# Holding back output transposes, moving an eviction to ScalarE and three subtractions to GpSimd in a one-core attention and gated-cosine kernel

## The chip, the core and the metric

The kernel runs on one core of one Trainium2 chip. A core has TensorE for matrix products (PE in the profile, its weight loads PEld), VectorE (DVE), ScalarE (ACT), GpSimd (POOL) and SyncE (SP), which here issues most of the DMAs. The engines run side by side, each works through its own instructions in the order in which the program gives them, and semaphores make one wait for another. The metric is the device time of a run in microseconds (us), the median of several runs; lower is better.

## The reference

Two parts follow each other. A recurrent cross attention lets 512 tokens and 32 state vectors of each of 8 heads read each other, for 8 batches. Its result, 544 rows for each batch and 4352 in all, goes through a layer with the activation h·cos(h):

```python
B, H, S, Ns, D = (8, 8, 512, 32, 64)
a     = softmax(scale * x @ state.T)        # (B, H, S, Ns)
xread = a @ state
a2    = softmax(scale * state @ x.T)        # (B, H, Ns, S)
sread = a2 @ x
attn_out = concatenate([xread, sread], axis=2)           # 512 + 32 rows for a batch
x = attn_out.transpose(0, 2, 1, 3).reshape(B * 544, 512)
h = x @ w_in          # (4352, 512) @ (512, 2048)
g = h * cos(h)
out = g @ w_out       # (4352, 2048) @ (2048, 512)
```

## The kernel before

The second layer works with transposed data: features lie on partitions, the 512 tokens of a batch in the free dimension. A *step* makes one tile of h, 128 of the 2048 features (f = 0 to 15) for one batch, and turns it into a tile of g. So a batch has 16 steps, and the 32 x 8 = 256 state rows follow in 16 steps at the end.

Two batches form a pair (n = 0 to 3), because the product g @ w_out is done for two batches at once with seven block products in place of eight. A pair has four phases of eight steps: phases 0 and 1 are the even batch, phases 2 and 3 the odd one, and i = 0 to 7 counts the steps of a phase. For this, sums and differences of g tiles are made as the tiles come. The g tiles of phases 0 to 2 are also made two at a time with seven products in place of eight (`seven`, from batch 2 on); phase 3 of each pair uses the plain form below.

```python
hps = ctx.enter_context(tc.tile_pool(name="hps", bufs=2, space=PSUM))
osb = ctx.enter_context(tc.tile_pool(name="osb", bufs=2))
NHELD = 3

def hidden(t):                       # L471: the hidden product
    t.hp = hps.tile([P, S], F32, name="h")[:, 0:t.n]
    for i in range(t.kn):
        nc.tensor.matmul(out=t.hp, lhsT=t.lhs(i), rhs=t.rhs(i), ...)

# h cos h: turns of h are rounded to whole ones, the rest goes through the sine
def gate(t):                         # L567, ScalarE
    nc.scalar.activation(t.q.bitcast(I32), t.hp, func=ACTF.Copy, bias=0.25)
def gate2(t):                        # L570, VectorE
    nc.vector.tensor_tensor(t.q, t.q.bitcast(I32), t.hp, op=ALU.subtract)
def gate3(t):                        # L573, ScalarE
    nc.scalar.activation(t.q, t.q, func=ACTF.Sin, bias=halfpi, scale=-TWO_PI)
def gate4(t):                        # L580, VectorE: g, and the last reader of h
    nc.vector.tensor_tensor(t.g, t.hp, t.q, op=ALU.mult)

def minus(pr, out, a, b, soon=False):        # L586
    engine = nc.vector if soon and pr.n else nc.gpsimd
    engine.tensor_tensor(out, a, b, op=ALU.subtract)

def plus(out, bank, ch, b):                  # L630, VectorE, reads a PSUM bank
    ...
def keep_product(out, bank):
    nc.scalar.activation(out.t[:, 0], acc[bank][0], func=ACTF.Copy, scale=TWO_PI)         # L635
    nc.vector.tensor_scalar(out.t[:, 1], acc[bank][1], TWO_PI, None, op0=ALU.mult)        # L637
```

A finished output stands transposed in a `held` buffer. `store` puts two closures into a list, and the loop over the steps takes one of them in each step:

```python
later = []
def store(b, half, src):
    def go(ch):
        ot = osb.tile([P, S], F32, name="ot")
        nc.vector.transpose(out=ot..., in_=src.t[:, ch]...)      # L651
        for q in range(P // 32):
            nc.sync.dma_start(out=rows[:, :, c0:c0 + 32], in_=ot[32 * q:32 * q + 32]...)   # L657
        src.done()
    later.extend([lambda: go(0), lambda: go(1)])

def sums(t):
    pr, i = t.pair, t.i
    pr.b[t.phase, i] = t
    if t.phase == 2:
        minus(pr, pr.b[0, i].g, t.g, pr.b[0, i].g, True)         # t1
    if t.phase == 3:
        minus(pr, pr.b[0, i].g, t.g, pr.b[0, i].g, True)
        minus(pr, pr.b[2, i].g, t.g, pr.b[2, i].g)

def output(t):                       # three steps after its tile
    ...
    if t.phase < 3 and pr.before and i % 3 < 2:
        pr.before.more(1)            # two products left over from the pair before
    ...
    if t.phase == 2:
        if product(MAIN, s1, pr.b[0, i], i):     # the fifth product; true after i = 7
            pr.p5 = Held()
            keep_product(pr.p5, MAIN)
    ...
```

The last of the products that the pair before left over comes with i = 4 of phase 2, in step 7 of the odd batch; then `plus` and `store` follow. At the same time the attention of the next batch is computed, as parts that a plan gives to the steps: for an odd batch b, the scores and `max1` in step 5, `spread1` (L339) and `shift` (L356) in step 6, `max2` (L349) and both exponentials (L360, L365) in step 7, sums (L333, L375, L376) and `spread1` (L339) in step 8, `norm1` (L386) in step 9. In step 11 `halves` (L493) makes sums for the next batch's hidden products, in step 12 `keep` (L419) follows. The main loop, cut:

```python
for step, t in enumerate(all_tiles):
    s = step % NF
    ...
    hidden(t)                        # or the form for two tiles
    ...
    go(0)                            # parts of the attention
    gate(t); gate2(t)
    go(1); go(3)
    gate3(t)
    ...
    if later:
        later.pop(0)()
    ...
    gate4(t)
    if t.pair is not None:
        sums(t)
    go(2); go(4)
    ...
    while len(line) >= (LAG if step >= 2 * NH else LAG + 1):     # LAG = 3
        output(line.pop(0))
    line.append(t)
```

Of the kernel before, what the change touches and what calls it, by code (L numbers as in the profile page):

```python
# [13 lines left out]
ACTF = mybir.ActivationFunctionType  # L14
# [3 lines left out]
TWO_PI = 2.0 * math.pi  # L18
# [3 lines left out]
def kernel(  # L22
# [8 lines left out]
    nc = tc.nc  # L31

    B, H, S, D = x.shape
# [9 lines left out]
    scale = 1.0 / math.sqrt(D)  # L43
# [23 lines left out]
    NH = NF // 2  # L67
# [58 lines left out]
    def load_state(half, queues):  # L126
        b = slice(4 * half, 4 * half + 4)
        for k in range(NK):
# [11 lines left out]
    acc = [[ops.tile([P, S], F32, name=f"o{m}{ch}") for ch in range(2)]  # L140
           for m in range(2)]
# [109 lines left out]
    class Attention:  # L251
# [126 lines left out]
        def sums(self):  # L378
            self.reduce1([self.z1[:, j] for j in range(2)], ALU.add)
            self.inverse(self.m1 if self.b == 0 else self.i12)  # L380
# [98 lines left out]
    def seven(t):  # L479
        return t.pair is not None and t.b > 1 and t.phase < 3  # L480
# [103 lines left out]
# [4 lines that stand above are left out]
    MAIN, SIDE = 0, 1  # L588
# [33 lines left out]
    def product(bank, w, g, i):  # L622
        for ch in range(2):
            nc.tensor.matmul(out=acc[bank][ch],  # L624
                             lhsT=w[:, i, P * ch:P * ch + P], rhs=g.g,
                             start=(i == 0), stop=(i == NH - 1))
        return i == NH - 1

    def plus(out, bank, ch, b):
        nc.vector.scalar_tensor_tensor(out=out.t[:, ch], in0=acc[bank][ch],  # L630
                                       scalar=TWO_PI, in1=b.t[:, ch],
                                       op0=ALU.mult, op1=ALU.add)

    def keep_product(out, bank):
        nc.scalar.activation(out.t[:, 0], acc[bank][0], func=ACTF.Copy,  # L635
                             scale=TWO_PI)
        nc.vector.tensor_scalar(out.t[:, 1], acc[bank][1], TWO_PI, None,  # L637
                                op0=ALU.mult)

    later = []  # L640
# [6 lines left out]
# [4 lines that stand above are left out]
            nc.vector.transpose(out=ot.rearrange("p (j i) -> p j i", i=32),  # L651
                                in_=src.t[:, ch].rearrange(
                                    "p (j i) -> p j i", i=32))
            rows = out[b * T:b * T + S, :].rearrange("(j t) d -> t j d", t=32)
            for q in range(P // 32):
                c0 = HD * half + P * ch + 32 * q
                nc.sync.dma_start(  # L657
                    out=rows[:, :, c0:c0 + 32],
                    in_=ot[32 * q:32 * q + 32].rearrange(
                        "p (j i) -> p j i", i=32))  # L660
# [5 lines that stand above are left out]
        pr, i = t.pair, t.i  # L666
        pr.b[t.phase, i] = t
        if t.phase == 2:
            minus(pr, pr.b[0, i].g, t.g, pr.b[0, i].g, True)
        if t.phase == 3:  # L670
            minus(pr, pr.b[0, i].g, t.g, pr.b[0, i].g, True)
            minus(pr, pr.b[2, i].g, t.g, pr.b[2, i].g)
# [6 lines left out]
    def free(t):  # L679
        g_free.append(t.slot)  # L680
# [18 lines left out]
    def output(t):  # L699
        if t.pair is None:  # L700
            state_output(t)
            return
        pr, i = t.pair, t.i
        if t.phase < 3 and pr.before and i % 3 < 2:
            pr.before.more(1)
        if t.phase == 0:
            if product(MAIN, a11, t, i):
                pr.u = Held()
                keep_product(pr.u, MAIN)
        if t.phase == 1:  # L710

            bank = MAIN if pr.before else SIDE
            if product(bank, a12, t, i):
                o = Held()
                for ch in range(2):
                    plus(o, bank, ch, pr.u)
                store(2 * pr.n, 0, o)
        if t.phase == 2:
            if product(MAIN, s1, pr.b[0, i], i):
                pr.p5 = Held()  # L720
                keep_product(pr.p5, MAIN)
        if t.phase == 3:
            last = product(SIDE, s4, t, i)
            free(t)
            if last:
                o = Held()
                for ch in range(2):
                    plus(o, SIDE, ch, pr.p5)
            product(MAIN, s2, pr.b[0, i], i)
            free(pr.b[0, i])  # L730
            if last:
                for ch in range(2):
                    plus(pr.u, MAIN, ch, pr.u)
                total(o, o, pr.u)
                store(2 * pr.n + 1, 0, o)
# [12 lines left out]
    def state_output(t):  # L748
        if t.n_th < NF - N_LAST:
            for i in range(2):  # L750
                state_product(t, i)
            t.last_pair.more(2)
            free(t)
            return
        kept_back.append(t)
        if len(kept_back) == N_LAST:
            t.last_pair.more(2 * N_LAST)
            for i in range(2):
                for u in kept_back:
                    state_product(u, i)  # L760
                state_store(i)
# [165 lines left out]
    for step, t in enumerate(all_tiles):  # L927
        s = step % NF
        if s == 0 and t.b < B:
            steps = plan(t.b)  # L930
        todo = [p[s] if t.b < B else [] for p in steps]

        def go(n):
            for p in todo[n]:
                part(*p)

        last, conv = conv_at.get(step - 1, -1), conv_at.get(step, -1)
        if step == B * NF + (0 if f64 else 8):
            fetch(N_LOADS + 2)
        if step == 4:  # L940
            warm(1, acc[MAIN][0])
        ahead = all_tiles[step + 1:step + 3]
        if seven(t):
            if t.f % 2 == 0:
                hidden_b(t)
                sums_b(t)
                if s == NF - 2 and seven(all_tiles[step + 2]):
                    halves(t.b + 1)
        elif step != 1:
            hidden(t)  # L950
        first = len(ahead) > 1 and seven(ahead[0]) and ahead[0].f % 2 == 0
        if first:
            if not seven(t):

                h = t.hp
                take_slot(t)
                nc.scalar.copy(t.g, h)
            hidden_a(*ahead)
        if step == 0:
            hidden(all_tiles[1])  # L960
            warm(3, acc[MAIN][0])
            gate(t)
            gate2(t)
            convert(3, "bcdf")
            convert(4, "1")
            go(0)
        else:
            go(0)
            if step == 5:
                states(1, acc[SIDE][1])  # L970
            if not (seven(t) and t.f % 2):
                gate(t)
            gate2(t)
            if step == 3:
                warm(4, acc[MAIN][0])
                part(0, "products", 1, SIDE)
            if first:
                sums_a(ahead[0])
            go(1)
            go(3)  # L980
            if step == 1:
                convert(4, "bcdf")
            elif last >= 0:
                convert(last, "bcdf")
            if conv >= 0 and not todo[1]:
                convert(conv, "1")
        gate3(t)
        if seven(t) and t.f % 2 == 0:
            gate(t.second)
        if step == 3:  # L990
            part(0, "products_kept", 1, SIDE)
        if later:
            later.pop(0)()
        for u, new in zip(all_tiles[step + 2:step + 4], (False, True)):
            if seven(u) and u.f % 2 == 0 and new_pair(u) == new:
                sw_sums(u)
        gate4(t)
        if conv >= 0 and todo[1] and step > 0:
            convert(conv, "1")
        if t.pair is not None:  # L1000
            sums(t)
        if step == 6:
            states_kept(1, acc[SIDE][1])
        go(2)
        if conv >= 0:
            convert(conv, "2")
        go(4)
        for u in all_tiles[step + 5:step + 6]:
            if seven(u) and new_pair(u):
                halves(u.b)  # L1010
        if step in block_at:
            blocks(*block_at[step])
        if t.pair is not None:
            sums2(t)
        while len(line) >= (LAG if step >= 2 * NH else LAG + 1):
            output(line.pop(0))
        line.append(t)
# [32 lines left out]
```

## Time and profile before

| quantity | value |
|---|---|
| device time, three runs | 764.83, 764.83, 766.66 us |
| median | 764.83 us |
| span of the profiled execution | 764.2 us |
| granted TensorE clock, mean | 0.997 |
| VectorE L580, g (h in PSUM) | 53 of mean 681 ns |
| L586 on GpSimd / on VectorE | 80 of mean 1433 ns / 48 of mean 697 ns |
| VectorE L651, output transposes | 32 of mean 693 ns |

The profile is one execution. A row gives line, engine and operation, what it writes and reads, how many there were and how long they took, and the idle time of the engine ahead of them with what ended it. A timeline's row has its start, its length, then the same. A 128x512 product in this data type is recorded as two passes, so the two products of one tile of h show as x4. The rows of matmuls are longer than their distance from start to start[...]. A wait for several semaphores is put down to the one that came last.

### The profile page before, as it was taken

The page shows a single profiled execution, that of the slowest core. Times are in us where ns is not written, and L with a number is a line of the kernel's source. Part 1 is how long each engine was busy: PE and PEld are TensorE (multiplying, and loading weights), DVE is VectorE, ACT ScalarE, POOL GpSimd, SP SyncE. Part 2 cuts the span into 40 slices and gives each one's busy share as a digit, 9 for nine tenths or more (in the row PEclk, how much of TensorE's full clock was granted, in tenths as well). Part 3 has the DMA queues.
Part 4 walks back from the last instruction along what each step waited for, and adds up shares of the span by engine and source line. Part 5 has one row for each costly group of instructions (what it writes and reads, how often), then busy time and mean ns, then how long its engine had stood idle before and what let it go on. Part 6 is the DMA issues. An engine that isn't in the chain of part 4 may idle for free.

```text
span 764.2 us, 8416 instructions
## 1 busy us (share of the span) xinstructions
PE 751.7 (98%) x2880; PEld 380.4 (50%) x2880; DVE 520.3 (68%) x862; ACT 316.3 (41%) x523; POOL 249.3 (33%) x258
## 2 busy tenths in 40 slices
PE   8998999999999999999999999999999999999997
PEld 3443443445555554445555553445555554455554
DVE  5778777836896788847886789747878676432431
ACT  3887844533254335333362335333443333212212
POOL 2354278777121210662221111751211206500200
PEclk9999999999999999999999999999999999999999
DMA  8595461050002510340105210420100115000021
GB/s 247 170 274 209 131 98 29 4 107 1 14 15 49 90 28 4 54 82 0 29 1 97 41 28 15 70 54 1 27 1 1 28 28 138 0 0 15 14 42 41
DMA packets 161962, 43.54 MB, mean 57 GB/s; under 512 B 153920, under 2 KB 153920, under 8 KB 161920
## 3 DMA queue, kind: packets, MB, share of 16 engines
q1 hardware_dynamic: 161024, 42.49, 25.7%
q10 hardware_dynamic: 768, 0.39, 0.2%
q8 instruction: 23, 0.38, 0.2%
q14 instruction: 19, 0.16, 0.1%
q0 software_dynamic: 128, 0.13, 0.1%
HBM read 34.08 MB, written 8.91 MB: 56 GB/s over the span
## 4 chain that ended last, share of the span: by engine, by line
PE 87%; DVE 7%; ACT 2%; issue 1%; DMA 1%; POOL 1%; SPq 0%; DVEq 0%; ACTq 0%; POOLq 0%
PE o L624 47%; PE h L514 14%; PE h L471 14%; PE at L319 4%; PE o L744 4%; PE at L409 2%; DVE xT L339 1%; PE o L319 1%; DVE q L570 1%; DVE g_all L580 1%; DVE i L333 1%; DMA g_all<-in_moe_w_in_dram 1%; ACT q L567 1%; PE at L392 1%; DVE aT L356 1%
## 5 line engine op out<-in xcount | busy, mean ns | idle before, releaser
L624 PE MATMUL o<-g_all,w_out 128*128 128x512 f32 x512 | 236.4, 598 | 0.4 <-POOL w_out L242 0.4
L624 PE MATMUL o<-g_all,s 128*128 128x512 f32 x384 | 177.3, 598 | 0.0
L586 POOL TENSOR_TENSOR g_all<-g_all 128x512 f32<-128x512 f32 x80 | 112.8, 1433 | 121.2 <-DVE g_all L580 121.2
L624 PEld LDWEIGHTS o<-g_all,w_out 128*128 128x128 f32 x512 | 93.8, 190 | 113.1 <-issue 108.4
L573 ACT ACTIVATE q<-q,halfpi 128x512 f32<-128x512 f32 (+1 forms) x144 | 100.8, 700 | 95.8 <-DVE q L570 95.6
L624 PEld LDWEIGHTS o<-g_all,s 128*128 128x128 f32 x384 | 70.8, 190 | 88.1 <-issue 82.1
L570 DVE TENSOR_TENSOR q<-q,h 128x512 f32<-128x512 int32 (+1 forms) x69 | 42.9, 621 | 103.6 <-ACT q L567 103.6
L471 PE MATMUL h<-aT,sw 128*128 128x512 f32 x224 | 107.2, 602 | 4.8 <-DVE g_all L580 4.3
L567 ACT ACTIVATE q<-g_all 128x512 int32<-128x512 f32 x75 | 46.8, 624 | 141.8 <-DVE g_all L560 141.4
L567 ACT ACTIVATE q<-h 128x512 int32<-128x512 f32 (+1 forms) x69 | 37.6, 545 | 131.0 <-PE h L471 131.0
L570 DVE TENSOR_TENSOR q<-q,g_all 128x512 f32<-128x512 int32 x75 | 52.7, 703 | 35.5 <-ACT q L567 35.5
L471 PEld LDWEIGHTS h<-aT,sw 128*128 128x128 f32 x224 | 41.8, 190 | 60.2 <-issue 45.0
L509 POOL TENSOR_TENSOR swS<-sw 128x128 f32<-128x128 f32 x35 | 17.4, 496 | 148.6 <-PE h L514 107.3
L580 DVE TENSOR_TENSOR g_all<-g_all,q 128x512 f32<-128x512 f32 x75 | 54.0, 720 | 14.5 <-ACT q L573 14.4
L580 DVE TENSOR_TENSOR g_all<-h,q 128x512 f32<-128x512 f32 (+1 forms) x69 | 42.8, 621 | 23.5 <-ACT q L573 23.1
L242 POOL TENSOR_TENSOR w_out<-w_out,s 128x1024 int32<-128x1024 int32 x10 | 23.9, 2390 | 77.6 <-DVE w_out L237 73.4
L509 POOL TENSOR_TENSOR swS<-sw,swS 128x128 f32<-128x128 f32 x35 | 18.3, 522 | 87.4 <-PE h L514 86.9
L514 PEld LDWEIGHTS h<-aT,sw 128*128 128x128 f32 x144 | 27.4, 190 | 34.4 <-issue 28.0
L514 PE MATMUL h<-aS,sw 128*128 128x256 f32 x144 | 43.1, 381 | 0.1
L514 PE MATMUL h<-aS,swS 128*128 128x256 f32 x144 | 42.8, 379 | 0.0
L514 PE MATMUL h<-aT,sw 128*128 128x256 f32 x144 | 42.8, 379 | 0.0
L586 DVE TENSOR_TENSOR g_all<-g_all 128x512 f32<-128x512 f32 x48 | 33.5, 697 | 1.6
(107 smaller groups left out, 886.3 us busy)
## 6 DMA issues: line engine op xcount, KB each, us to landing
out_dram<-ot SPq DMA_DIRECT2D x132, 64.0 KB, 2.0
g_all<-in_moe_w_out_dram SPq DMA_DIRECT2D x8, 1024.0 KB, 5.0
g_all<-in_moe_w_in_dram SPq DMA_DIRECT2D x6, 1024.0 KB, 5.3
xT<-in_x_dram SPq DMA_DIRECT2D x96, 64.0 KB, 2.3
x_b<-in_x_dram SPq DMA_DIRECT2D x24, 256.0 KB, 4.5
x_b<-in_x_dram SPq DMA_DIRECT2D x16, 128.0 KB, 3.8
g_all<-in_moe_w_in_dram SPq DMA_DIRECT2D x4, 512.0 KB, 5.9
x_b<-in_moe_w_out_dram SPq DMA_DIRECT2D x1, 1024.0 KB, 6.1
```

The source lines that it names most:

```text
L242: nc.gpsimd.tensor_tensor(bits, bits, e, op=ALU.add)
L319: nc.tensor.matmul(out=(to or at)[j][Ns * k:Ns * k + Ns, 0:n], lhsT=w[D * j:D * j + D, self.b, Ns * k:Ns * k + Ns], rhs=r(slice(D * j, D * ...
L471: nc.tensor.matmul(out=t.hp, lhsT=t.lhs(i), rhs=t.rhs(i), start=(i == 0), stop=(i == t.kn - 1))
L509: engine.tensor_tensor(o, x1, x2, op=op)
L514: nc.tensor.matmul(out=out, lhsT=w, rhs=r, start=True, stop=True)
L567: nc.scalar.activation(t.q.bitcast(I32), t.hp, func=ACTF.Copy, bias=0.25)
L570: nc.vector.tensor_tensor(t.q, t.q.bitcast(I32), t.hp, op=ALU.subtract)
L573: nc.scalar.activation(t.q, t.q, func=ACTF.Sin, bias=halfpi, scale=-TWO_PI)
L580: nc.vector.tensor_tensor(t.g, t.hp, t.q, op=ALU.mult)
L586: engine.tensor_tensor(out, a, b, op=ALU.subtract)
L624: nc.tensor.matmul(out=acc[bank][ch], lhsT=w[:, i, P * ch:P * ch + P], rhs=g.g, start=(i == 0), stop=(i == NH - 1))
L744: nc.tensor.matmul(out=acc[MAIN][i], lhsT=t.g[:, P * i:P * i + P], rhs=w_out[:, :, t.f, :], start=(t.n_th == 0), stop=(t.n_th == NF - 1))
```

## The change

It moves work away from VectorE around the middle of batches 3, 5 and 7 in three places. (1) In steps 7 to 11 of these batches nothing is taken from `later`, so the transposes and stores that would fall there wait until step 12. (2) In pairs 1 to 3, both halves of the fifth product are evicted by ScalarE; before, VectorE did the second half. (3) In pairs 1 to 3, the subtraction t1 of phase 2 is done by GpSimd for i = 5, 6, 7; before, by VectorE for all i. No computation is added or left out. It is meant to keep VectorE's queue short where the next batch's attention, the first pairs of plain tiles and the end of the fifth product meet.

```diff
-    def keep_product(out, bank):
-        nc.scalar.activation(out.t[:, 0], acc[bank][0], func=ACTF.Copy,
-                             scale=TWO_PI)
+    def keep_product(out, bank, scalar=False):
+
+        for ch in range(2 if scalar else 1):
+            nc.scalar.activation(out.t[:, ch], acc[bank][ch], func=ACTF.Copy,
+                                 scale=TWO_PI)
+        if scalar:
+            return
         nc.vector.tensor_scalar(out.t[:, 1], acc[bank][1], TWO_PI, None,
                                 op0=ALU.mult)
...
         if t.phase == 2:
-            minus(pr, pr.b[0, i].g, t.g, pr.b[0, i].g, True)
+            minus(pr, pr.b[0, i].g, t.g, pr.b[0, i].g, i < 5)
...
                 pr.p5 = Held()
-                keep_product(pr.p5, MAIN)
+                keep_product(pr.p5, MAIN, pr.n > 0)
...
-        if later:
+
+
+        full = t.b % 2 == 1 and 1 < t.b < B and NH - 1 <= s < NH + 4
+        if later and not full:
             later.pop(0)()
```

## Prediction

> **What bounds the kernel now.** I first read the page's busy times.
>
> ```profile
> PE 751.7 (98%) x2880; PEld 380.4 (50%) x2880; DVE 520.3 (68%) x862; ACT 316.3 (41%) x523; POOL 249.3 (33%) x258
> ```
>
> TensorE is busy 98% of the span, so a change that touches only VectorE, ScalarE and GpSimd can only win time in which TensorE stands still. A matmul's row overlaps its successor's, so I looked for such time in the distance between starts, not in the busy share. The timeline of TensorE alone gives the distance: four passes of a 128x512 matmul follow each other in 1.72 us, 0.43 us each. Next came the waits of TensorE over the whole run:
>
> ```profile
> PE h L471 <- DVE g_all L580: 4.3, 6, 1.9
> ```
>
> The hidden product (L471) waits for the product g (L580, the last reader of an `h` buffer), six times. Asked in stretches, the same view puts two of them at 290 to 320 us and two at 460 to 482 us, the same place in batches 3 and 5; the rest lies ahead of 160 us, in batches 0 and 1. There TensorE's timeline (start, length, what, in brackets idle time and releaser) reads, for batch 3:
>
> ```profile
> 302.78 1.98 PE L624 MATMUL o<-g_all,s 128*128 128x512 f32 x4
> 304.95 1.98 PE L471 MATMUL h<-aT,sw 128*128 128x512 f32 x4 [0.18 <-DVE g_all L580]
> 306.77 1.04 PE L392 MATMUL at<-ident,xT 128*128 128x128 f32 x8
> 307.65 1.88 PE L624 MATMUL o<-g_all,s 128*128 128x512 f32 x4
> 310.32 1.98 PE L471 MATMUL h<-aT,sw 128*128 128x512 f32 x4 [0.79 <-DVE g_all L580]
> ```
>
> and for batch 7, where no next batch's attention is computed:
>
> ```profile
> 639.68 1.88 PE L624 MATMUL o<-g_all,s 128*128 128x512 f32 x4
> 641.40 1.88 PE L471 MATMUL h<-aT,sw 128*128 128x512 f32 x4
> ```
>
> In batch 7 the hidden product follows exactly 1.72 us after the four passes ahead of it: nothing is lost. In batch 3 four passes from 307.65 end at 309.37, but step 11's product starts at 310.32: 0.95 us. Step 10's starts at 304.95 where 302.78 + 1.72 + 0.10 = 304.60 was possible (that group of four is itself 0.10 longer): 0.35 us. Both groups of L471 are 0.10 longer than in batch 7, a restart after the stop. So each of batches 3 and 5 loses 0.35 + 0.95 + 2 x 0.10 = 1.50 us here, and batch 7 nothing. Batch 5 shows the same offsets (472.24 and 477.61).
>
> Why g is late is in VectorE's timeline of batch 5, steps 5 to 10, cut to what matters:
>
> ```profile
> 456.07 0.69 DVE L586 TENSOR_TENSOR g_all<-g_all 128x512 f32<-128x512 f32 x1
> ...
> 461.05 0.69 DVE L586 TENSOR_TENSOR g_all<-g_all 128x512 f32<-128x512 f32 x1
> ...
> 465.57 0.69 DVE L586 TENSOR_TENSOR g_all<-g_all 128x512 f32<-128x512 f32 x1
> ...
> 470.96 0.65 DVE L651 STREAM_TRANSPOSE ot<-held 128x512 f32<-128x512 f32 x1
> 471.54 0.65 DVE L580 TENSOR_TENSOR g_all<-h,q 128x512 f32<-128x512 f32 x1
> ...
> 474.57 1.79 DVE L386 TENSOR_TENSOR aT<-aT,xT 128x1024 f32<-128x1024 f32 x1
> 476.28 0.70 DVE L651 STREAM_TRANSPOSE ot<-held 128x512 f32<-128x512 f32 x1
> 476.91 0.65 DVE L580 TENSOR_TENSOR g_all<-h,q 128x512 f32<-128x512 f32 x1
> ```
>
> Each L580 that TensorE awaits stands directly behind an output transpose (L651), in a queue with next to no idle time: VectorE is busy 9.57 of the 10.50 us from 470.5 to 481.
>
> **What the Trainium skill says.** "Perfetto Trace Analysis", section Optimization Strategy, says to find the gaps of the engine to be optimized and what frees them, and that a recurring gap can mean too few SBUF or PSUM buffers. The trace agrees: `h` has two buffers, and step s waits for the g of step s - 2. "TensorE: Matmul & The Clock Gate", section on the 16× 32×32 array, says ScalarE's and VectorE's queues are strict FIFO; so a transpose ahead of L580 delays it though nothing needs it. "GPSIMD Engine Reference", section 3.1, has a two-input elementwise operation 1.96 times slower there than on VectorE. Here L586 has a mean of 1433 ns on GpSimd and 697 on VectorE, 2.06 times. "SBUF — State Buffer", section Who interferes with whom, says that a VectorE instruction with two SBUF inputs contends with a GpSimd instruction that reads SBUF. The trace agrees: L386 takes from 1.21 to 2.08 us, and a 128x256 subtraction (L493) from 0.41 up to 1.49.
>
> **The change part by part.**
>
> *Transposes held back.* `later` holds back the pair before's last store from its last product. In batches 3, 5, 7 it was done in steps 8 and 9; now it is done in steps 12 and 13. The order of VectorE's instructions confirms it: the two transposes now stand ahead of the L580 of steps 12 and 13. Removed from the crowded place: 2 x 0.65 us = 1.3. The same work is added later, where there is room: in batch 5, L580 of step 12 starts at 489.82, and the next `h` buffer it frees is used at 496.82; step 13's L580 runs at 495.24 for a product at 501.97. 0.65 us later costs nothing there.
>
> *Three subtractions to GpSimd.* L586 for i = 5, 6, 7 of phase 2 leaves VectorE: 3 x 0.69 = 2.07 us in each of three pairs. GpSimd is idle there: its next operation after the sums ending at 447.6 is at 472.27, with 24.64 us of waiting. Each takes some 1.4 us there, and its result is used three steps later (i = 7: finished near 466.5, its product at 474.94). Not all 2.07 us count: after i = 5, L560 waits for its matmuls anyway. The one for i = 6 counts: L356, L570, the sine, the exponentials and the gate of step 8 hang on it in a row, with ScalarE idle 3.01 us for that L570. The one for i = 7 then lets L630 go before the gate.
>
> *Fifth product.* VectorE's L637 (0.68 us, at 481.12 in batch 5) goes and ScalarE has two of 0.60 instead of one. ScalarE's next gate (480.49) slips by 0.6, but L570, which needs it, stood behind L637 until 481.72 anyway. Neutral.
>
> Followed through, for batch 5: step 8's gate on ScalarE comes 0.68 us earlier (467.22 for 467.90), table load and sine follow, ending at 469.84. VectorE's reductions and reciprocal end at 470.4 at the latest, so with no transpose L580 of step 8 starts near 470.3 and ends near 470.95. TensorE can use it at 472.24 - 0.35 = 471.9: margin 0.9, the wait of step 10 is gone. Then L586 ends at 471.6, L339 at 472.8, L570 of step 9 at 473.4, L386 (still beside GpSimd, so 1.8 us) at 475.1, and L580 of step 9 ends near 475.7 instead of 477.56. TensorE, now 0.45 us earlier, wants it at 476.66 - 0.45 = 476.2: margin 0.5, the wait of step 11 is gone too.
>
> The sum: 2 batches x 1.50 = 3.0 us; batch 7 gives 0 because it has no wait. 764.83 - 3.0 = 761.8. I take 761.9, as a small rest may remain at step 11.
>
> **The rivals.**
>
> *A shorter wait at step 11 stays.* Its margin of 0.5 us is an estimate out of several rows. For it: GpSimd's earlier pair of subtractions may overlap L386 more fully, and L386 has been seen at 2.08. Against it: both release from the same L580, so they move together. Half of step 11's wait left would be 2 x 0.5 us: 762.9.
>
> *Contention eats the gain.* GpSimd's three subtractions now run beside VectorE. For it: L493 tripled beside GpSimd. Against it: beside these three stand mostly operations with a PSUM input (L559, L560, L356, L630), which keep their 0.4 to 0.7 us in the trace while GpSimd works. Only one L570 with two SBUF inputs falls under the second, which I put at up to 0.25 us, inside the margins. At the worst all of the gain for one batch is gone: 763.3.
>
> *A new wait at steps 12 and 13*, or a store that blocks loads on its queue. For it: step 11 and 12 hold four L493 and four L419, and the moved stores now stand behind the next tokens' loads. Against it: the 7 us of slack just named, and the stores now follow the loads rather than precede them; in batch 7 the last two weight loads (at 639.30) do slip behind the stores, to about 655 to 660, but they are used only some five steps into the state tokens that begin near 667. If I missed one: 0.7 us in each of three batches, 764.
>
> *More than the visible waits.* TensorE's other distances in these batches are the 0.10 us steps behind the 64x32 and 128x64 groups, which the change doesn't touch. I see no further gain.
>
> **Range and chances.** Full success gives 761.8, the partial cases 762.9 to 764. The times before were 764.83, 764.83 and 766.66, so a median can sit some tenths off. I say 761.9, with 761.0 to 764.1 for 8 in 10. 2% would be 15.3 us, five times the time that TensorE loses here: within 2% has 0.98, faster 0.01, slower 0.01.
>
> **What would show it.** Right: no wait of L471 for L580 in batches 3 and 5, L471 of steps 10 and 11 starting 1.72 to 1.82 us after the group ahead of it; L651 gone from steps 8 and 9 and standing in 12 and 13; POOL's long wait of 24.64 us cut by three operations; 12 fewer VectorE instructions (3 L637, 9 L586); the state part beginning about 3 us earlier. Batch 7's distances unchanged. Wrong: a wait of L471 of 0.3 us or more left at step 11 (margins too optimistic), a new one at steps 12 to 14, or L570 and L580 of steps 6 to 8 lengthened well past 0.7 us beside GpSimd.

## The result and the profile after

| | before | changed |
|---|---|---|
| device time, median of six | 765.52 us (764.58 to 766.66) | 762.45 us (761.84 to 764.70) |
| ratio | | 0.9965, 95% interval 0.9948 to 0.9982 |
| span of the profiled execution | 764.2 us | 762.9 us |
| VectorE busy / ScalarE / GpSimd | 520.3 / 316.3 / 249.3 us | 513.5 / 317.8 / 261.6 us |

The ratio times 765.52 us is a gain of 2.7 us (1.4 to 4.0). The prediction said 761.9 us with 761.0 to 764.1, from 764.83: a gain of 2.9.

In the changed kernel lines from L635 on are numbered a few higher: the output transpose L651 is now L655, ScalarE's eviction L635 is L637. First, the waits of TensorE in the changed kernel, the whole run:

```profile
PE h L471 <- DVE g_all L580: 2.4, 2, 1.9
```

Six such waits became two. From 160 us to the end the list of TensorE's waits is empty, where the kernel before had four there; the two left are both in batch 0 (the prediction placed them in batches 0 and 1). The timeline of TensorE at the same place of batch 3 (start, length, what):

```profile
304.50 1.98 PE L624 MATMUL o<-g_all,s 128*128 128x512 f32 x4
306.33 1.88 PE L471 MATMUL h<-aT,sw 128*128 128x512 f32 x4
...
308.92 1.88 PE L624 MATMUL o<-g_all,s 128*128 128x512 f32 x4
310.63 1.88 PE L471 MATMUL h<-aT,sw 128*128 128x512 f32 x4
```

Step 10's hidden product starts 1.83 us after the group ahead of it and step 11's 1.71, and no row has idle time behind it. Both groups of L471 are back at 1.88. Now VectorE's timeline of batch 5, steps 6 to 9, cut:

```profile
461.44 1.28 DVE L356 TENSOR_TENSOR aT<-at,xT 128x512 f32<-128x512 f32 x2
462.64 0.78 DVE L570 TENSOR_TENSOR q<-q,g_all 128x512 f32<-128x512 int32 x1
...
470.56 0.37 DVE L376 RECIPROCAL i<-i 128x34 f32<-128x34 f32 x1
470.84 0.63 DVE L580 TENSOR_TENSOR g_all<-h,q 128x512 f32<-128x512 f32 x1
...
473.85 1.80 DVE L386 TENSOR_TENSOR aT<-aT,xT 128x1024 f32<-128x1024 f32 x1
475.57 0.68 DVE L580 TENSOR_TENSOR g_all<-h,q 128x512 f32<-128x512 f32 x1
```

No transpose stands ahead of either awaited L580. GpSimd's timeline of the same stretch has the three subtractions, 1.27 us each, in what was an idle time of 24.64 us:

```profile
456.33 1.27 POOL L586 TENSOR_TENSOR g_all<-g_all 128x512 f32<-128x512 f32 x1 [8.48 <-DVE g_all L580]
461.60 1.27 POOL L586 TENSOR_TENSOR g_all<-g_all 128x512 f32<-128x512 f32 x1 [4.00 <-DVE g_all L580]
465.50 1.28 POOL L586 TENSOR_TENSOR g_all<-g_all 128x512 f32<-128x512 f32 x1 [2.62 <-DVE g_all L580]
```

**A finer measure than the time.** The times scatter by 2 to 3 us, as much as the effect. So I also measure stretches on TensorE: from the start of the scores (L319 on xT), done in step 5 of a batch for the next one, to the same place one batch later, 16 steps. The span of the change's profile needs this: it is only 1.3 us shorter than the one of before, because it has 1.7 us more ahead of 122 us, where the change does nothing:

| stretch, from the scores done in one batch to those done in another | before | changed |
|---|---|---|
| start to batch 1 | 120.72 us | 122.44 us |
| batch 1 to batch 3 | 164.80 | 164.80 |
| batch 3 to batch 4 | 85.31 | 83.81 |
| batch 4 to batch 5 | 81.98 | 81.98 |
| batch 5 to batch 6 | 85.30 | 83.81 |
| batch 6 to the state tokens | 129.03 | 129.04 |

Batches 3 and 5 give 1.50 and 1.49 us; batch 7, which lies in the last row, gives nothing. Part of the 1.7 us shows in two stretches of time of the two profiles (time, busy time of PE, PEld, DVE, ACT, POOL, granted clock, DMA share, GB/s). Before:

```profile
7.70:11.20 3.50, 3.25 (x28) 1.59 (x28) 1.66 (x4) 1.71 (x3) 0.00 (x0) 1.00 1.05 366
73.60:80.00 6.40, 6.40 (x26) 1.95 (x25) 5.83 (x10) 5.23 (x8) 1.27 (x1) 0.73 0.45 160
```

Changed:

```profile
7.70:11.20 3.50, 3.44 (x18) 2.66 (x24) 1.49 (x4) 1.71 (x3) 0.00 (x0) 0.51 1.05 365
73.60:80.00 6.40, 5.20 (x22) 1.43 (x23) 5.20 (x9) 5.33 (x11) 2.36 (x1) 0.73 0.49 164
```

In the changed kernel's profiled execution the clock was halved in one more stretch, at 7.7 us. As an estimate, 3.5 us at 0.51 of the clock cost up to 1.7 us; but only 0.9 us were lost by the first scores, the rest between there and the scores done in batch 1, so that this stretch accounts for all of it is not shown. Such stretches differ from run to run, whatever the kernel; the stretches from batch 1 on that a run does not touch repeat to 0.03 us.

### The profile page after: what moved, and what is told of

Read it like the earlier page. It is cut to its first block, busy times and chain, and to the rows that moved or that the text cites. A ratio compares the mean times of both kernels' runs of the same rounds, so it can differ in the third digit from the quotient of the medians.

```text
span 762.9 us, 8427 instructions
## 1 busy us (share of the span) xinstructions
PE 751.9 (99%) x2880; PEld 381.5 (50%) x2880; DVE 513.5 (67%) x850; ACT 317.8 (42%) x526; POOL 261.6 (34%) x267
## 4 chain that ended last, share of the span: by engine, by line
PE 92%; DVE 3%; ACT 2%; DMA 1%; POOL 1%; issue 1%; SPq 0%; DVEq 0%; ACTq 0%; POOLq 0%
PE o L624 50%; PE h L471 15%; PE h L514 14%; PE at L319 5%; PE o L748 4%; PE at L409 2%; PE o L319 1%; PE at L392 1%; DMA x_b<-in_x_dram 1%; DVE w_out L237 0%; ACT q L567 0%; DVE i L333 0%; PE o L805 0%; DVE g_all L580 0%; POOL g_all L586 0%
## 5 line engine op out<-in xcount | busy, mean ns | idle before, releaser
L586 POOL TENSOR_TENSOR g_all<-g_all 128x512 f32<-128x512 f32 x89 | 124.8, 1423 | 107.2 <-DVE g_all L580 107.2
L570 DVE TENSOR_TENSOR q<-q,h 128x512 f32<-128x512 int32 (+1 forms) x69 | 42.9, 622 | 107.3 <-ACT q L567 107.2
L471 PE MATMUL h<-aT,sw 128*128 128x512 f32 x224 | 106.2, 597 | 2.9 <-DVE g_all L580 2.4
L567 ACT ACTIVATE q<-g_all 128x512 int32<-128x512 f32 x75 | 46.9, 625 | 142.2 <-DVE g_all L560 141.8
L567 ACT ACTIVATE q<-h 128x512 int32<-128x512 f32 (+1 forms) x69 | 37.8, 547 | 132.0 <-PE h L471 131.9
L570 DVE TENSOR_TENSOR q<-q,g_all 128x512 f32<-128x512 int32 x75 | 52.9, 705 | 36.1 <-ACT q L567 36.1
L471 PEld LDWEIGHTS h<-aT,sw 128*128 128x128 f32 x224 | 41.9, 190 | 56.6 <-issue 45.7
L580 DVE TENSOR_TENSOR g_all<-g_all,q 128x512 f32<-128x512 f32 x75 | 54.2, 723 | 14.4 <-ACT q L573 14.3
L580 DVE TENSOR_TENSOR g_all<-h,q 128x512 f32<-128x512 f32 (+1 forms) x69 | 42.8, 621 | 22.3 <-ACT q L573 21.4
L242 POOL TENSOR_TENSOR w_in<-w_in,s 128x1024 int32<-128x1024 int32 (+1 forms) x10 | 19.3, 1932 | 37.9 <-DVE w_in L237 22.0
```

The source lines that it names most:

```text
L242: nc.gpsimd.tensor_tensor(bits, bits, e, op=ALU.add)
L471: nc.tensor.matmul(out=t.hp, lhsT=t.lhs(i), rhs=t.rhs(i), start=(i == 0), stop=(i == t.kn - 1))
```

## The experiments

My theory: VectorE's queue ahead of the g of steps 8 and 9 (L580) is what TensorE waited for, and only what leaves that queue counts. Rival A: the transposes alone did it. Rival B: VectorE's total work falls, and that helps wherever it falls. Rival C: ScalarE's share is needed. All runs, with the stretches of batches 3 and 5 from the traces; each ratio is to the kernel before as measured beside that run:

| run | stretch of batch 3, 5 (us) | median time | ratio to before, interval |
|---|---|---|---|
| before | 85.31, 85.30 | | |
| changed | 83.81, 83.81 | 762.45 | 0.9965 (0.9948 to 0.9982) |
| transposes held back alone | 84.11, 84.11 | 763.54 | 0.9967 (0.9957 to 0.9978) |
| three subtractions alone | 84.68, 84.68 | 764.75 | 0.9988 (0.9979 to 0.9997) |
| two subtractions alone (i = 6, 7) | 84.69, 84.68 | 763.84, one run | |
| eviction alone | 85.30, 85.58 | 765.87 | 0.9999 (0.9988 to 1.0011) |
| all but the eviction | 83.80, 83.80 | 762.89 | 0.9961 (0.9947 to 0.9975) |
| changed, one transpose back in step 9 | 84.07, 84.37 | 764.17, one run | |
| subtractions of i = 0, 1, 2 | 86.84, 86.85 | 768.97 | 1.0044 (1.0029 to 1.0060) |
| the same, GpSimd's order swapped | 85.60, 85.59 | 766.73, one run | |
| subtractions of i = 3, 4 | 85.31, 85.31 | 769.13, one run | |

The time of a single run says little here: the 769.13 us lost 3.1 us against the kernel before ahead of the scores done in batch 1 (123.86 for 120.72 us), with two stretches at half the clock, and none from there on.

### Each part alone

The transposes held back, on the kernel before:

```diff
+        full = t.b % 2 == 1 and 1 < t.b < B and NH - 1 <= s < NH + 4
-        if later:
+        if later and not full:
             later.pop(0)()
```

> The kernel before with the transposes held back alone. Theory (two queues of VectorE work stand ahead of the awaited g, and each part's share is what it takes off that queue): the wait of step 10 goes; at step 11 g comes 0.34 to 0.63 us later than with all three parts, which had 0.18 (batch 5) to 0.46 us (batch 3) to spare, so a wait of about 0.2 us, with its restart 0.3, is left in each batch: gain 2.4 us of 3.0. Rival A (the transposes alone are the cause): no wait left, 3.0. Rival B (the subtractions are the cause, or the total of VectorE's work): under 1.

Measured: 84.11 in both, 1.20 us gained in each, 2.4 in all, and the time agrees (0.9967 of 765.95 is 2.5 us). TensorE's timeline of batch 3, step 11:

```profile
307.01 1.88 PE L624 MATMUL o<-g_all,s 128*128 128x512 f32 x4
308.94 1.98 PE L471 MATMUL h<-aT,sw 128*128 128x512 f32 x4
```

The product starts 1.93 us after the group ahead, 0.21 later than it could, and its own group is 0.10 longer. No wait is booked, because the matmul's row still runs; only the starts show it. Rival A falls in its pure form: 0.30 us is left in each batch without the other parts. So does rival B: this run takes no work off VectorE, it only moves it, and gains the most of any part.

The three subtractions alone:

```diff
-            minus(pr, pr.b[0, i].g, t.g, pr.b[0, i].g, True)
+            minus(pr, pr.b[0, i].g, t.g, pr.b[0, i].g, i < 5)
```

> The kernel before with the three subtractions on GpSimd alone. Theory: step 10's wait goes or is under 0.1 us; at step 11 both transposes (1.3 us) still stand ahead, against 0.18 to 0.46 us to spare, so 0.85 to 1.1 us of wait are left there: gain 0.3 to 0.6 in each batch, 0.6 to 1.2 in all. Rival A (transposes alone): 0. Rival B (subtractions, or the total of VectorE's work: 6.2 us of it go here, 3.9 in the run with the transposes held): more than the run with the transposes held back.

Measured: 84.68, a gain of 0.63 in each batch. Batch 3, step 11:

```profile
307.28 1.88 PE L624 MATMUL o<-g_all,s 128*128 128x512 f32 x4
309.77 1.13 PE L471 MATMUL h<-aT,sw 128*128 128x512 f32 x2 [0.61 <-DVE g_all L580]
```

Step 10's wait is gone, 0.77 us are left at step 11. The run takes more work off VectorE than the one before it (9 x 0.69 = 6.2 us against two transposes of 0.65 moved in each of three batches) and gains half as much. The two parts overlap: 1.20 + 0.63 is more than 1.50, since step 10's wait goes with either.

With `i < 6` in place of `i < 5`, only i = 6 and 7 move:

> The kernel before with the subtractions of i = 6 and 7 alone on GpSimd. The prediction said that the one for i = 5 does not count, because L560 waits for its matmuls behind it anyway. Theory: both stretches as with all three on GpSimd, 84.68 us within 0.1. Rival (each counts its 0.69 us): 0.2 to 0.7 us longer.

84.69 and 84.68: the same as with three, to 0.01 us. The subtraction of i = 5 on VectorE costs nothing.

The eviction by ScalarE alone:

```diff
-    def keep_product(out, bank):
-        nc.scalar.activation(out.t[:, 0], acc[bank][0], ...)
+    def keep_product(out, bank, scalar=False):
+        for ch in range(2 if scalar else 1):
+            nc.scalar.activation(out.t[:, ch], acc[bank][ch], ...)
+        if scalar:
+            return
...
-                keep_product(pr.p5, MAIN)
+                keep_product(pr.p5, MAIN, pr.n > 0)
```

> The kernel before with the fifth product's second half evicted by ScalarE alone. Theory: L637 comes after both awaited g, so both waits stay as before, 1.50 us in each of batches 3 and 5: gain 0. Rival B (the total of VectorE's work): 2.0 us off VectorE, a gain of some tenths.

85.30 in batch 3, 85.58 in batch 5, time 0.9999. No gain; the 0.28 us more in batch 5 is step 10's wait, 0.46 in place of 0.18 in TensorE's waits there. It comes ahead of batch 5's own eviction, but behind batch 3's. It begins at ScalarE's gate of step 6 in batch 5 (L567), which waits for VectorE's L560. First this run, then the run with all but the eviction:

```profile
456.97 0.69 DVE L560 TENSOR_TENSOR g_all<-g_all,h 128x512 f32<-128x512 f32 x1
458.03 0.63 ACT L567 ACTIVATE q<-g_all 128x512 int32<-128x512 f32 x1 [5.16 <-DVE g_all L560]
```

```profile
454.43 0.69 DVE L560 TENSOR_TENSOR g_all<-g_all,h 128x512 f32<-128x512 f32 x1 [0.44 <-PE h L514]
455.22 0.63 ACT L567 ACTIVATE q<-g_all 128x512 int32<-128x512 f32 x1 [4.88 <-DVE g_all L560]
```

The gate starts 0.37 us behind the end of L560 here and 0.10 there. In all five runs in which ScalarE evicts both halves it is 0.37 to 0.39 us in batch 5; in the other eight, and in batch 3 of every run, it is 0.09 to 0.10. So the delay goes with the eviction's move, and why it does is not shown. The reverse, all but the eviction:

> The changed kernel with the fifth product evicted as before. Theory: the eviction comes behind both awaited g, so the gain is that of the change: both stretches 83.81 us, 2.5 to 3.0 us in the time. Rival (ScalarE's share is needed): a wait of some tenths at step 11 or later.

83.80 twice. Rival C falls; the eviction's move gives nothing. It takes nothing from the change's time either, but it takes 0.30 us from what batch 5 has to spare: between the end of L580 of step 9 and the start of the product that awaits it lie 0.48 us without the eviction's move and 0.18 with it.

### A dose at the deciding place

The changed kernel, with one transpose back in step 9:

```diff
-        full = t.b % 2 == 1 and 1 < t.b < B and NH - 1 <= s < NH + 4
+        full = t.b % 2 == 1 and 1 < t.b < B and NH - 1 <= s < NH + 4 and s != NH + 1
```

> The changed kernel with one of the two transposes done in step 9 again, ahead of its awaited g; the other stays in step 12. A dose of 0.65 us at the point whose margin decides. Theory: the g of step 9 had 0.18 us (batch 5) to 0.46 us (batch 3) to spare, so 0.2 to 0.5 us of wait come back at step 11, with a restart of 0.1: each stretch from the scores of batch 3 (or 5) to the next batch's is 0.3 to 0.6 us longer than with the change (83.81), step 10 stays free. Rival (the margin is large, the gain is the subtractions'): 83.81 unchanged.

84.07 and 84.37: 0.26 and 0.56 us lost. TensorE's timeline of batch 5:

```profile
473.45 1.88 PE L624 MATMUL o<-g_all,s 128*128 128x512 f32 x4
475.63 1.98 PE L471 MATMUL h<-aT,sw 128*128 128x512 f32 x4 [0.30 <-DVE g_all L580]
```

The transpose put back makes the awaited L580 of batch 5 end 0.58 us later, counted from the scores. Of it 0.46 come out as a late start (2.18 - 1.72), and the restart adds 0.10. The rest, 0.12, is what there was to spare. The change's own trace has 0.18 (L580 ends at 476.25, L471 starts at 476.43), of which 0.05 pass between the end of g and the start of a product that has awaited it. In batch 3 the trace has 0.46, and 0.17 came out as a late start. The change is just large enough.

### VectorE's work taken off elsewhere

As many subtractions, but those of i = 0, 1, 2:

```diff
-            minus(pr, pr.b[0, i].g, t.g, pr.b[0, i].g, True)
+            minus(pr, pr.b[0, i].g, t.g, pr.b[0, i].g, i > 2)
```

> As many subtractions on GpSimd as in the change, but those of i = 0, 1, 2 in place of 5, 6, 7; transposes and eviction as before. VectorE's total falls by the same 6.2 us. Theory: the queue ahead of the awaited g starts at step 6 and has idle time ahead of it, so nothing is gained: 0, both waits 1.50 us in each of batches 3 and 5. Rival B (the total): the same gain as with i = 5, 6, 7.

It was a miss for both theories: 1.5 us *slower* in each of batches 3 and 5, 3 us in the time. Rival B is refuted, but mine had said 0. Step 10's wait is the same 0.18 as before; step 11's rose to 1.37 and 1.38. The timelines of VectorE and GpSimd in batch 5, step 8, show where it comes from:

```profile
473.00 0.65 DVE L580 TENSOR_TENSOR g_all<-h,q 128x512 f32<-128x512 f32 x1
...
473.74 1.26 POOL L586 TENSOR_TENSOR g_all<-g_all 128x512 f32<-128x512 f32 x1 [25.17 <-DVE g_all L580]
473.76 1.79 DVE L586 TENSOR_TENSOR g_all<-g_all 128x512 f32<-128x512 f32 x1
```

These are phase 3's subtractions for i = 0. VectorE's takes 1.79 us in place of 0.69 and ends 0.55 us behind GpSimd's. In the kernel before, VectorE started first:

```profile
472.22 0.69 DVE L586 TENSOR_TENSOR g_all<-g_all 128x512 f32<-128x512 f32 x1
472.27 1.77 POOL L586 TENSOR_TENSOR g_all<-g_all 128x512 f32<-128x512 f32 x1 [24.64 <-DVE g_all L580]
```

So in these runs whoever starts first works at its pace, and the other is stretched: VectorE's by 1.10 us beside 1.26 of GpSimd's, GpSimd's by 0.50 beside 0.69 of VectorE's. VectorE starts later here because its subtraction now has two semaphores to wait for: its own g, and GpSimd's t1 on the same tile. The trace has an extra semaphore instruction of 21 ns ahead of L586, and L586 starts 0.10 us behind the end of L580 in place of 0.03. GpSimd won by 0.025 us, in all nine such cases (i = 0, 1, 2 of three pairs).

I tested this by letting GpSimd do its two operations of phase 3 in the other order for these i. Its first then needs VectorE's result, and it can't start ahead:

```diff
     if t.phase == 3:
         minus(pr, pr.b[0, i].g, t.g, pr.b[0, i].g, True)
-        minus(pr, pr.b[2, i].g, t.g, pr.b[2, i].g)
+        if not pr.n or i > 2:
+            minus(pr, pr.b[2, i].g, t.g, pr.b[2, i].g)
...
         minus(pr, pr.b[1, i].g, pr.b[1, i].g, pr.b[0, i].g)
+        if pr.n and i < 3:
+            minus(pr, pr.b[2, i].g, t.g, pr.b[2, i].g)
```

> The kernel with the subtractions of i = 0, 1, 2 on GpSimd, and in phase 3 for the same i GpSimd's two subtractions in the other order, so that its first needs VectorE's L586 and cannot start ahead of it. Nothing else differs. Theory: VectorE's L586 took 1.79 us in place of 0.69 because a second semaphore to wait for let GpSimd's operation start 0.03 us ahead of it[...]; with the order swapped L586 takes 0.69 to 0.81 us, and the stretches fall from 86.84 to 85.3, as in the kernel before (85.31). Rival (the time comes from GpSimd's other load in steps 0 to 2): 86.8 stays.

Batch 5, step 8 and 9:

```profile
472.75 0.69 DVE L586 TENSOR_TENSOR g_all<-g_all 128x512 f32<-128x512 f32 x1
473.52 2.50 POOL L586 TENSOR_TENSOR g_all<-g_all 128x512 f32<-128x512 f32 x2 [25.95 <-DVE g_all L586]
475.10 2.01 DVE L386 TENSOR_TENSOR aT<-aT,xT 128x1024 f32<-128x1024 f32 x1
```

L586 is back at 0.69 in steps 8 and 9 (0.96 in step 10), and the stretches fall from 86.84 to 85.60 and from 86.85 to 85.59. 0.3 us above the kernel before are left; L386, now beside more of GpSimd's work, takes 2.01 us in place of 1.79, which accounts for 0.2 of it, and the later start of L586 in step 8 for 0.07. So swapping the order gave back 1.24 of the 1.53 us, which the load that GpSimd has in steps 0 to 2 (the expectation's rival) does not explain.

A control takes i = 3 and 4, whose second wait falls into step 11, behind both awaited g:

```diff
-            minus(pr, pr.b[0, i].g, t.g, pr.b[0, i].g, True)
+            minus(pr, pr.b[0, i].g, t.g, pr.b[0, i].g, i not in (3, 4))
```

> The kernel before with the subtractions of i = 3 and 4 on GpSimd: VectorE's work in steps 3 and 4 falls by 1.4 us, ahead of the place, and the second wait that this gives L586 falls into step 11, behind both awaited g. Theory: both waits stay, stretches of batches 3 and 5 at 85.3 us as before; the L586 of step 11 takes 1.79 us and costs nothing. Rival (VectorE's work anywhere in the batch counts): up to 1.4 us shorter.

85.31 twice, both waits as before (0.18 and 0.80 by the trace), and the L586 of step 11 took its 1.79 us at 319.83 without any cost. So 1.4 us less work on VectorE in steps 3 and 4, ahead of the queue that starts at step 6, is worth nothing. The theory holds, and the change's choice of i = 5, 6, 7 avoids the trap: in steps 13 and 14 of batch 5 it is L580 that waits for GpSimd's semaphore too, so L586 has no second wait of its own, and in step 15 it has none either; it took 0.70, 0.69 and 0.69 us.

### The same remedy in batch 0

The longest wait left is 1.9 us in batch 0: step 11's hidden product waits for step 9's L580, which stands behind a weight conversion (L234, L237). I put the conversion behind it, and the next step's sums (L333, L375, L376) behind theirs:

```diff
-            elif last >= 0:
+            elif last >= 0 and step != 9:
                 convert(last, "bcdf")
...
         gate4(t)
+        if step == 9:
+            convert(last, "bcdf")
...
-            x_dve[s[5]].append((b, "sums"))
+            (y_dve if b == 1 else x_dve)[s[5]].append((b, "sums"))
```

> The changed kernel, with the same remedy at the one long wait left, in batch 0 (step 9 to 11): the weight conversion (L234, L237: 1.9 us on VectorE) and the sums (L333, L375, L376) are done behind the awaited g instead of ahead of it. Theory: the wait of 2.1 us at one hidden product goes; two steps later the next g comes only 1.0 us after TensorE is ready, since ScalarE's exponentials and table load are ahead of its sine: 0.8 to 1.1 us gained on the change, ratio to before 0.995. If the half-clock stretch of 3.4 us that some runs show right behind this wait goes with it, up to 1.5 us more in these runs. Rival (other engines' work hides it, or the next conversion comes too late): no gain.

A miss. 763.79 us, ratio 0.9975 (0.9964 to 0.9985), no better than the change; the stretch from the scores done in batch 0 to those done in batch 1 (the two batches' scores that the expectation below calls those of batch 0 and 2) is 63.67 us. The run with all but the eviction, which has no half-clock stretch there either, has 62.21. Counted from the scores, step 11's product did come 1.94 us earlier than in that run and step 12's 0.74, but step 13's 0.12 later, and from batch 1 on everything 1.46 later. VectorE's and TensorE's timelines:

```profile
76.42 0.69 DVE L580 TENSOR_TENSOR g_all<-h,q 128x512 f32<-128x512 f32 x1 [1.35 <-ACT q L573]
77.03 1.29 DVE L333 TRANSPOSE_TENSOR_REDUCE i<-aT 128x16 f32<-128x512 f32 x2
...
97.85 1.98 PE L471 MATMUL h<-aT,sw 128*128 128x512 f32 x4 [1.25 <-DVE g_all L580]
```

In the 1.35 us in which VectorE now waits for the sine, the sums used to run. Behind that, they push the rest of the queue back. To part the two moves, the conversion alone:

> The changed kernel with the weight conversion of batch 0's step 9 behind the awaited g, and the sums in their old place. In the run that moved both, VectorE idled 1.35 us for a sine where the sums used to stand, and everything behind them came 1.5 us later. Theory: with the sums back, the hidden product of step 9 keeps its 1.9 us gain, the next one 0.7 us, and the g of step 9 is no later than before; so the stretch from the scores of batch 0 to those of batch 2, 62.2 us without a half-clock stretch, becomes 61.5, or stays at 62.2 if a later conversion on ScalarE sets step 14 anyway; never 63.7. Rival (moving the conversion itself, through its later fetch of the next weights, was what cost): 63.0 or more.

(Step 9 stands here for the product that awaits step 9's g.) 762.29 us, 0.9950 (0.9931 to 0.9968), stretch 62.45: 1.22 of the 1.46 us of loss are gone, so the sums were the cause of that, and the gain is gone too. Step 11's product comes 1.56 us earlier than without the move and that of batch 1's step 0 0.24 later: something else sets the pace by then, and which of the conversions it is I did not part. Against the change (0.9965) and the change without its eviction (0.9961) the intervals overlap widely; none of the versions is shown to be faster than the change.

## Why the prediction was right

- *Waits of 1.50 us in each of batches 3 and 5, none in batch 7.* Right to 0.01 us: 1.50, 1.49 and 0.
- *Step 10.* "Margin 0.9": 0.94 in batch 3 (L580 ends at 305.39, L471 starts at 306.33), 0.65 in batch 5. *Step 11.* "Margin 0.5": 0.46 and 0.18. The mechanism held. The chain that the prediction followed for batch 5 is nearly exact for the run without the eviction: counted from the scores, the two L580 end at 18.14 and 22.91 us there, and the prediction's 470.95 and 475.7 are 18.13 and 22.88. With the eviction they ended 0.30 later, which the prediction did not have. That batch 5 stayed free of a wait all the same was luck in part: about 0.13 us were to spare.
- *i = 5 does not count, i = 6 and 7 do.* Shown: 84.69 against 84.68.
- *Fifth product neutral.* Right for the time, both ways, but not for the margin, as just said. ScalarE's next gate came at 479.67 and VectorE's L570 at 480.31 then waited 0.41 us for it, where it used to stand behind L637.
- *Contention.* L570 beside GpSimd took 0.78 us in place of 0.68, 0.10 more where I had allowed 0.25; L356 and L630, with PSUM inputs, kept 1.28 for two. GpSimd's own three took 1.27 us each, not the 1.4 that I had put. "Whoever starts first" was not in my prediction; the change escapes it, and I had not seen that it could have failed by that.
- *Steps 12 and 13.* The transposes run there at 488.44 and 492.38 in batch 5, with no wait of TensorE.
- *The last two weight loads* slip behind the stores, the first of them from 639.30 to 656.67 (predicted 655 to 660), as SyncE's timeline has it. It cost nothing: from the last scores to the end both profiles take 226.1 us:

```profile
590.35 66.22 SPq L661 DMA_DIRECT2D out_dram<-ot  x24
656.67 0.43 SPq L197 DMA_DIRECT2D x_b<-in_moe_w_out_dram  x1
```

- *The shared ports.* The Trainium skill, "SBUF — State Buffer", section Who interferes with whom, calls the pair of ports that VectorE and GpSimd share an exclusive lock, and says that the order of issue decides which of the two blocks. The runs agree: 0.69 against 1.79 us for one subtraction, by a start order of 0.025 us. The delay, 1.79 - 0.69 = 1.10 us, is a little less than the 1.26 that GpSimd took. Undisturbed, GpSimd took 1.27 us for what VectorE does in 0.69.

## What to carry to other kernels

Where one engine is nearly full, look at the distances between its starts for the few places where it stands still, and at the in-order queue of the engine it waits for: only what leaves that queue ahead of the awaited instruction counts, and the same work taken off earlier, ahead of that queue, was worth nothing. Before moving work off, see whether it filled a wait that is there anyway, and whether moving it gives a later instruction one more semaphore. The margin that is left says how robust the gain is: here some 0.13 us in batch 5. And a part of a change that gives nothing can still take from that margin, as the eviction did.

## What was not expected of the hardware

- Of two elementwise operations on VectorE and GpSimd that both read SBUF, the one that starts first keeps its time (0.69 or 1.26 us) and the other is stretched (to 1.77 on GpSimd, 1.79 on VectorE). One more semaphore to wait for came with a start 0.07 us later, which turned this order and cost 1.5 us in a batch.
- In 9 of the 13 profiled executions TensorE's clock was halved early in the run for one or two stretches of 3.4 us, around 8 us or around 75 us, behind places where it had stood still. In kernels that leave batch 0 alone, the stretch from its scores to batch 1's took 62.1 to 62.3 us without the second one and 63.4 to 63.9 with it. The Trainium skill, "TensorE: Matmul & The Clock Gate", Part 1, has the clock at half after an idle window of about 3.4 us. The traces agree in length and share (0.51 in the window above), but the standstill ahead of the one at 75 us was only 1.95 us long, and four runs with the same standstill kept the full clock behind it (transposes alone, two subtractions alone, eviction alone, all but the eviction).
